# The order of work on Pool in the first half of an attention and mixture-of-experts kernel: gate bias and q spreads ahead of later loads, the k sort evacuations shared out anew, and expert pieces from unit 16

## The chip, the cores and the metric

The kernel runs on one core of a Trainium2 chip. Its time is device microseconds; the figure of a kernel is the median of its runs. The core has five engines that work side by side, each in the order of its own instructions: TensorE (PE in the profile), VectorE (DVE), ScalarE (ACT), GpSimd (POOL) and SyncE (SP). Transfers between the chip's main memory and the on-chip memory go over DMA queues; those that change the type from f32 to bf16 on the way are issued by Pool, as are the scatters of single rows.

## The reference

The input is q, k, v of shape (4, 8, 768, 64), a table `sort_net` of 8 x 8 for each of the 32 heads, and the weights of a gate and of eight experts. Cut to what matters:

```python
P = sort_net
for _ in range(5):                       # rows, then columns, are normalised
    P = exp(P - max(P)); P /= sum(P, -1); P /= sum(P, -2)
k_sorted = einsum('bhij,bhjcd->bhicd', P, k_b)   # 8 blocks of 96 rows are mixed
v_sorted = einsum('bhij,bhjcd->bhicd', P, v_b)
scores = scale * q_b @ k_sorted.T                # inside each block of 96
attn   = softmax(scores);  attn_out = attn @ v_sorted

x      = attn_out as (3072, 512)
logits = x @ w_gate + modality_bias[modality_id]
e_idx  = argmax(logits);  gate_w = softmax(logits)[e_idx]
out    = gate_w * (relu(x @ w1[e_idx]) @ w2[e_idx])   # one expert for each row
```

## The kernel before

Heads are handled in two groups of 16 (two batches each); g is 0 for the first half and 1 for the second. The whole attention is 32 *units*: unit u has one head number (u % 8) of two batches and four of the eight blocks. A unit is scores (sc), exponential (attnT), product with v (op), and division into the row buffer xb. While units run, other work is hung on them: q is spread into an interleaved layout (`spread_q`, tile q_il), transposed on TensorE (`tq_pe`, tile tq) and copied (tile qT); the rows of a finished head pair are transposed (`gate_T`, tile gt), copied (xTg), multiplied with the gate (`gate_L`, tile lg) and added up (lacc). The first of the four gate products of a group of rows also takes the gate bias, tile biasm, which `gate_bias` computes on Pool:

```python
def spread_q(g, hq, eng=None):      # two copies of 128x768, one for each of two heads
    t = q_in(g, hq // 2).rearrange(...)
    il = q_il[hq % 2].rearrange(...)
    for z in range(2):
        (eng or nc.vector).tensor_copy(il[:, z], t[...])
...
def gate_bias():
    nc.gpsimd.tensor_scalar(modN, modF, -1.0, 1.0, ALU.mult, ALU.add)
    ...
    nc.gpsimd.tensor_tensor(biasm, modF.broadcast_to([BLK, NTL, E]), bb(1), ALU.mult)
    nc.gpsimd.tensor_tensor(tmp, modN.broadcast_to([BLK, NTL, E]), bb(0), ALU.mult)
    nc.gpsimd.tensor_tensor(biasm, biasm, tmp, ALU.add)
...
def gate_L(m, c):
    lg = mipsum.tile([BLK, 8, E], FP32, tag="mi", name=f"lg{m}_{c}")
    for t in range(8):
        nc.tensor.matmul(lg[:, t], xTg[c % 2][:, t], wgp[:, c], start=True, stop=True)
    ...
    if c == 0:
        nc.vector.tensor_tensor(la..., lg..., bm, ALU.add)      # bm is a view of biasm
    else:
        nc.vector.tensor_tensor(la, la, lg, ALU.add)
```

PSUM results are copied out either by ScalarE or by VectorE. Which of the two is decided when the program is written, by a running account of work given to each: `use` adds to the account, `pick` takes the engine that would be done first, `copy_out` is a copy by the engine picked.

```python
def pick(act, dve):
    top = max(busy)
    for z in range(2):
        busy[z] = max(busy[z], top - 3.0)
    z = 0 if busy[0] + act <= busy[1] + dve else 1
    busy[z] += (act, dve)[z]
    return z == 0
...
def sort_k(g, c0, kind):            # "mi": 8 columns in a one-bank tile; "sc", "op": 16 in two banks
    ...                             # matmuls on k_raw, into tile ka
    copy_out(dst, acc..., *((0.6, 0.7) if kind == "mi" else (1.03, 1.23)))
```

The order of the first half, as it stands in the program:

```python
use(dve=0.5)
home_pick()                          # 13 small VectorE operations
mod_rows()
kinds = [s_, o_] + [m_] * 8 + ([m_] * 4 + [o_]) * 2 + [m_] * 4
g0 = jobs(0, kinds)
for f, g, x0, kd in g0[:10]:         # the k sort of the first half
    f(g, x0, kd)
scores(0); expo(0); mod_T()
load_k(1, 0); load_k(1, 1)           # k of the second half, into the buffer of the first
home_map()                           # its last part on Pool: perm_mult(BTp, ...)
gate_w()                             # Pool
spread_q(0, 1, nc.gpsimd)
use(dve=-busy[1], act=-busy[0])
for n, (f, g, x0, kd) in enumerate(g0[10:]):   # the v sort of the first half
    f(g, x0, kd)
    if n == 3:
        scores(1); expo(1)
load_v(1)
spread_q(0, 2, nc.gpsimd)
load_q(1, 0, 4); load_w(0, parts=(0,)); load_q(1, 4, 4); load_w(0, parts=(1,))
make_upper_triangular(nc, maskUT, val=1.0, diag=False)
...
prep_q(2); av(0); prep_q(3)          # prep_q: transposes of q for a unit, and their copy
```

Then the loop over the units. The lists A1 and A2 hold what is hung on a unit:

```python
at2(2, lambda: (spread_q(0, 3, nc.gpsimd), gate_bias()))
at2(3, make_bd, 1)
at2(4, late_consts)
# k and v sort of the second half: 12 and 16 jobs on units 8 to 15
for m in range(3):
    at2(8 * m + 9, place, m)         # choose expert places of 8 row tiles, scatter the rows
    at2(8 * m + 11, table_x, m)      # table of slots; x of a slot is loaded, transposed, into xT
at2(12, late_w1)                     # weights of the second expert, after x of slots 0 and 1

def pace(u):
    return (0, 0) if u < 17 else (1, u % 2)

for u in range(2, 32):
    p1, p2 = pace(u)
    scores(u); expo(u)
    run_pieces(p1)
    for f, a in A1.get(u, []): f(*a)
    av(u - 1); prep_q(u + 2); prep_s(u + 3)
    run_pieces(p2)
    for f, a in A2.get(u, []): f(*a)
run_pieces(1); av(31); run_pieces(1); gate_T(3, 3); run_pieces(1); gate_L(3, 3); choose(3)
run_pieces(1); place(3); run_pieces(1); table_x(3); run_pieces(1000)
```

A *piece* is a part of an expert's work on a slot of 256 rows: four pieces of eight matmuls for the first layer (tile hp) and two of eight for the second (tile yp). Twelve slots of six pieces and a last, smaller one make up the second stage of the kernel, and some of them are woven into the units of the second half.

Of the kernel before, what the change touches and what calls it, by code (L numbers as in the profile page):

```python
# [17 lines left out]
def kernel(  # L18
# [13 lines left out]
    nc = tc.nc  # L32
# [58 lines left out]
    def q_in(g, hh):  # L91
        base = q_in1 if g else v_sb[1].rearrange("p x d -> p (x d)")
        return base[:, hh * 3072:(hh + 1) * 3072]
# [15 lines left out]
    def load_k(g, part):  # L109
        cs = slice(part * RW // 2, (part + 1) * RW // 2)  # L110
        nc.gpsimd.dma_start(out=k_raw[:, cs], in_=k_src[g * 128:(g + 1) * 128, cs])

    def load_v(g):
        nc.gpsimd.dma_start(out=v_in, in_=v_src[g * 128:(g + 1) * 128])

    def load_q(g, h0, nh):
        t = q_in(g, h0 // 4).rearrange("p (r h f) -> p r h f", r=2, h=4)
        z = h0 % 4
        for par in range(2):
            nc.gpsimd.dma_start(out=t[:, par, z:z + nh], in_=q[2 * g + par, h0:h0 + nh]  # L120
                                .rearrange("h (p t) d -> p h (t d)", t=6))

    def spread_q(g, hq, eng=None):
        t = q_in(g, hq // 2).rearrange("p (r h t d) -> p r h t d", r=2, h=4, t=6)
        il = q_il[hq % 2].rearrange("p (h t r d) -> p h t r d", h=2, t=6, r=2)
        for z in range(2):
            (eng or nc.vector).tensor_copy(il[:, z], t[:, :, (hq % 2) * 2 + z].rearrange("p r t d -> p t r d"))  # L127
# [62 lines left out]
    def perm_mult(dst, srcs, nm):  # L190
        eng = nc.gpsimd
        tmp = small.tile([128, 4, E, E], FP32, tag="ptmp", name=f"ptmp{nm}")
        a = bass.AP(tensor=srcs.tensor, offset=srcs.offset, ap=[srcs.ap[0], srcs.ap[1], [0, E], srcs.ap[2]])
        p_ = bass.AP(tensor=perm.tensor, offset=perm.offset, ap=[perm.ap[0], [0, 4], perm.ap[1], perm.ap[2]])
        eng.tensor_tensor(tmp, a, p_, ALU.mult)
        for w in (4, 2):
            eng.tensor_tensor(tmp[:, :, :, 0:w], tmp[:, :, :, 0:w], tmp[:, :, :, w:2 * w], ALU.add)
        eng.tensor_tensor(dst.rearrange("p r (e o) -> p r e o", o=1), tmp[:, :, :, 0:1], tmp[:, :, :, 1:2], ALU.add)
# [32 lines left out]
    def tq_pe(u):  # L231
        h = u % 8
        src = q_il[(h // 2) % 2].rearrange("p (h t f) -> p h t f", h=2, t=6)[:, h % 2]
        tp = mipsum.tile([128, 6, 128], BF16, tag="mi", name=f"tq{u}")
        for t in range(6):
            nc.tensor.transpose(tp[:, t], src[:, t], ident)  # L236
        tq[u] = tp

    def tq_out(u, eng):
        g, h = u // 16, u % 8  # L240
        qT = qTb[g][:, h * 768:(h + 1) * 768].rearrange("p (i t r) -> p i t r", i=NB, t=6)
        eng(qT, tq.pop(u).rearrange("p t (i r) -> p i t r", r=16))
# [55 lines left out]
    def home_map():  # L298
        nc.vector.tensor_tensor_scan(cs_, ones8, oth, 0.0, ALU.mult, ALU.add)
        nc.vector.scalar_tensor_tensor(cs_, cs_, 1.0, oth, ALU.add, ALU.mult)  # L300
        nc.vector.tensor_tensor(cs_, cs_, ohB, ALU.add)
        hb = bass.AP(tensor=cs_.tensor, offset=cs_.offset, ap=[cs_.ap[0], [0, E], cs_.ap[1]])
        nc.vector.tensor_tensor(perm, hb, sF8.broadcast_to([128, E, E]), ALU.is_equal)
        perm_mult(BTp, BT, "b")
        nc.gpsimd.tensor_copy(etab, BTp[0:1, 3])
# [6 lines left out]
    def mod_rows():  # L312
        src = modI.rearrange("b (r t w) -> b t r w", r=16, t=6)[:, :, :, 0]
        nc.gpsimd.tensor_copy(modB, src)
# [8 lines left out]
    def gate_w():  # L323
        perm_mult(wgf, wg_sb, "w")
        nc.gpsimd.tensor_copy(wgp, wgf)

    def gate_bias():
        nc.gpsimd.tensor_scalar(modN, modF, -1.0, 1.0, ALU.mult, ALU.add)

        def bb(r):  # L330
            t = BTp[0:BLK, r]
            return bass.AP(tensor=t.tensor, offset=t.offset, ap=[t.ap[0], [0, NTL], t.ap[1]])
        tmp = small.tile([BLK, NTL, E], FP32, tag="btmp", name="btmp")
# [3 lines that stand above are left out]
# [3 lines left out]
    def use(act=0.0, dve=0.0):  # L340
        busy[0] += act
        busy[1] += dve
# [8 lines that stand above are left out]
# [28 lines left out]
    def jobs(g, kinds):  # L379
        res, c0, d0 = [], 0, 0  # L380
        for kd in kinds:
            if c0 < BLK:
                res.append((sort_k, g, c0, kd))
                c0 += 8 if kd == "mi" else 16
            else:
                res.append((sort_v, g, d0, kd))
                d0 += 4 if kd == "mi" else 8
        assert c0 == BLK and d0 == D
        return res
# [3 lines left out]
    def unit(u):  # L393
        return u // 16, (u // 8) % 2, u % 8
# [6 lines left out]
    def prep_q(u):  # L401
        if 2 <= u < 32 and not (u // 8) % 2:
            tq_pe(u)
            tq_out(u, nc.scalar.copy if pick(0.8, 0.56) else nc.vector.tensor_copy)
# [23 lines left out]
    def av(u):  # L428
        g, hf, h = unit(u)
        xt = xb[(u // 8) % 2]  # L430
        op = opsum.tile([128, 2, 512], FP32, tag="op", name=f"op{u}")
        ov = op[:, :, 0:4 * (D + 1)].rearrange("p r (j x) -> p r j x", x=D + 1)
        for par in range(2):
            for j in range(4):
                i = hf * 4 + j
                c0 = (par * 4 + j) * BLK
                nc.tensor.matmul(ov[:, par, j], attnT[u % 2][:, c0:c0 + 128],  # L437
                                 v_sb[g][0:BLK, par * 64 + h * 8 + i, 0:D + 1], start=True, stop=True)
        rs = small.tile([BLK, 2, 4, 1], FP32, tag="rs", name=f"rs{u}", bufs=2)
        nc.vector.reciprocal(rs, ov[0:BLK, :, :, D:D + 1])  # L440
        nc.vector.tensor_tensor(xt[:, :, h * D:(h + 1) * D].rearrange("p (r j) d -> p r j d", r=2),  # L441
                                ov[0:BLK, :, :, 0:D], rs.broadcast_to([BLK, 2, 4, D]), ALU.mult)
        use(dve=0.92)
# [171 lines left out]
    def zero_block():  # L615
        ins = nc.sync.dma_start(out=xs_dram[ZR:ZR + PR].rearrange("(t p) w -> p t w", t=2), in_=zsrc2)
        in_xs_group(ins.ins)
        pads.append(ins.ins)
# [125 lines left out]
    m_, s_, o_ = "mi", "sc", "op"  # L744
# [15 lines left out]
    use(dve=0.5)  # L760
    home_pick()
    mod_rows()
    kinds = [s_, o_] + [m_] * 8 + ([m_] * 4 + [o_]) * 2 + [m_] * 4
    g0 = jobs(0, kinds)
    for f, g, x0, kd in g0[:10]:
        f(g, x0, kd)
# [3 lines left out]
    load_k(1, 0)  # L770
    load_k(1, 1)
    home_map()
    gate_w()
    spread_q(0, 1, nc.gpsimd)
    use(dve=-busy[1], act=-busy[0])
    for n, (f, g, x0, kd) in enumerate(g0[10:]):
        f(g, x0, kd)
# [2 lines left out]
            expo(1)  # L780
    load_v(1)
    spread_q(0, 2, nc.gpsimd)
    load_q(1, 0, 4)
    load_w(0, parts=(0,))
    load_q(1, 4, 4)
# [1 line left out]
    make_upper_triangular(nc, maskUT, val=1.0, diag=False)  # L787
    nc.gpsimd.iota(zpad.bitcast(I32)[:, Dm // 2:Dm // 2 + 1], pattern=[[0, 1]], base=SKIP, channel_multiplier=0)
    zero_block()
    prep_q(2)  # L790
    av(0)
    prep_q(3)

    st = {"tab": -1, "x": 0, "l1": 0, "done": 0, "pos": 0}

# [21 lines left out]
    def at1(u, f, *a):  # L817
        A1.setdefault(u, []).append((f, a))

    def at2(u, f, *a):  # L820
        A2.setdefault(u, []).append((f, a))
# [7 lines left out]
    for m in range(4):  # L829
        for c in range(4):  # L830
            u = 8 * m + 2 * c + 3
# [5 lines left out]
                at1(u, gate_L, m, c)  # L837
        if m < 3:
            at1(8 * m + 9, choose, m)
    at2(2, lambda: (spread_q(0, 3, nc.gpsimd), gate_bias()))  # L840
    at2(3, make_bd, 1)
    at2(4, late_consts)
    k_at = [8] * 3 + [9] * 3 + [10] * 4 + [11] * 2
# [1 line left out]
    for u, (f, g, x0, kd) in zip(k_at + v_at, jobs(1, [m_] * 28)):  # L845
        at2(u, f, g, x0, kd)
    for m in range(3):
        at2(8 * m + 9, place, m)
        at2(8 * m + 11, table_x, m)
    at2(12, late_w1)  # L850

# [14 lines left out]
    def run_pieces(n):  # L866
        for _ in range(n):
            if st["pos"] >= len(pieces):
                return
            f, a = pieces[st["pos"]]  # L870
            if (f is mL1 and a[0] >= st["x"]) or (f is last_L1 and SL >= st["x"]):
                return
            f(*a)
            if f is mL1 and a[1] == 3:
                st["l1"] = a[0] + 1
            if f is mL2 and a[1] == 1:
                st["done"] = a[0] + 1
            x_try()
            st["pos"] += 1

    def pace(u):
        return (0, 0) if u < 17 else (1, u % 2)

    for u in range(2, 32):
        p1, p2 = pace(u)
# [10 lines left out]
            f(*a)  # L896
    run_pieces(1)
    av(31)
    run_pieces(1)
    gate_T(3, 3)  # L900
    run_pieces(1)
    gate_L(3, 3)
    choose(3)
    run_pieces(1)
    place(3)
    run_pieces(1)
    table_x(3)
    run_pieces(1000)
    assert st["pos"] == len(pieces)
# [74 lines left out]
```

The softmax here doesn't subtract the row's maximum and nothing guards it: scores larger than these inputs give would overflow.

## Time and profile before

| what | value |
|---|---|
| time, median of three runs | 243.31 us (243.28 to 244.02) |
| span of the profiled execution, first to last instruction | 207.0 us |
| mean granted TensorE clock | 0.867 of full speed |
| TensorE busy | 166.8 us, 81% of the span |
| VectorE busy | 102.1 us, 49% |
| ScalarE busy | 92.6 us, 45% |
| Pool busy | 83.5 us, 40% |
| moved by DMA | 27.66 MB, mean 134 GB/s |

The profile has the busy time of each engine, a picture of the span in 40 equal slices, and groups of instructions by line of the kernel, engine and operation. A name like "tq<-ident,q_il" gives the tile that is written and those that are read, so L236 is the transposes of q, L437 the product with v, L450 `gate_T`, L456 `gate_L`, L366 the k sort, L375 the v sort, L683 and L706 the two expert layers; on Pool L127 is `spread_q` and L328 to L336 are `gate_bias`; on VectorE L462 is the addition that takes biasm, and L441 the division into xb. The list of waits has, for an engine and a line, what it waited for, in microseconds in total, how often, and the longest. A timeline gives the start, the duration, and in square brackets how long the engine sat idle before and what released it. A table of windows has the busy time of each engine in a stretch, and near its end the granted TensorE clock, the DMA share and GB/s.

### The profile page before, as it was taken

How to read it: one execution, taken by the hardware profiler on the slowest of the kernel's cores; microseconds unless marked ns; L12 is line 12 of the kernel's file. 1: busy time of each engine (PE TensorE's matmuls, PEld its weight loads, DVE VectorE, ACT ScalarE, POOL GpSimd, SP SyncE). 2: the span in 40 equal slices, each digit the busy share in tenths (PEclk: the TensorE clock that was granted, in tenths of full speed). 3: DMA queues.
4: the chain of work that ended last, by engine and by line, in shares of the span. 5: the costliest groups of instructions: out<-in, count | busy, mean ns of one | idle time of the engine just before them, and what ended most of it. 6: DMA issues, size and time to landing. Idle time of an engine off the chain costs nothing.

```text
span 207.0 us, 5130 instructions
## 1 busy us (share of the span) xinstructions
PE 166.8 (81%) x2034; PEld 121.8 (59%) x2045; DVE 102.1 (49%) x333; ACT 92.6 (45%) x148; POOL 83.5 (40%) x118
## 2 busy tenths in 40 slices
PE   6395497438899998999978999889999999999100
PEld 2135496327698887768657586648676767654000
DVE  5969377255484866864638453572222322223000
ACT  2035368325575797759435674434232223232000
POOL 7901377930007603177241773257631313132300
PEclk9859679755555799999999999999999999999955
DMA  4999999999993326998550226963577321212200
GB/s 54 207 228 205 194 221 196 204 186 211 205 190 81 88 54 57 165 181 215 152 153 3 77 80 184 177 172 110 165 186 187 83 103 51 101 55 101 62 2 0
DMA packets 30160, 27.66 MB, mean 134 GB/s; under 512 B 18831, under 2 KB 25775, under 8 KB 29872
## 3 DMA queue, kind: packets, MB, share of 16 engines
q0 software_dynamic: 11792, 23.10, 51.0%
q1 hardware_dynamic: 18336, 4.16, 11.3%
q8 instruction: 18, 0.29, 0.6%
q14 instruction: 14, 0.11, 0.2%
HBM read 27.35 MB, written 10.52 MB: 183 GB/s over the span
## 4 chain that ended last, share of the span: by engine, by line
PE 60%; issue 10%; POOL 9%; DVE 9%; DMA 4%; ACT 2%; POOLq 0%; DVEq 0%
PE yp L706 20%; PE hp L683 18%; PE gt L450 4%; DMA kvb<-in_k_dram 4%; PE sc L418 3%; PE lg L456 3%; PE op L437 3%; PE ka L366 3%; DVE xb L441 2%; POOL q_il L127 2%; PE va L375 2%; POOL q_in L120 1%; ACT v_sb L353 1%; PE tq L236 1%; PE ypl L736 1%
## 5 line engine op out<-in xcount | busy, mean ns | idle before, releaser
L683 PE MATMUL hp<-xT,w 128*128 128x256 bf16 x384 | 47.3, 273 | 0.1
L527 POOL DMA_INDIRECT xs_scratch<-xb,dest x32 | 29.6, 926 | 38.8 <-issue 37.9
L697 POOL DMA_INDIRECT out_dram<-kvb,idg x25 | 24.5, 982 | 42.9 <-DVE kvb L695 22.0
L683 PEld LDWEIGHTS <-w 128*128 128x128 bf16 x384 | 36.1, 98 | 7.4
L424 ACT ACTIVATE attnT<-sc 96x768 bf16<-96x768 f32 x32 | 25.9, 808 | 10.4 <-PE sc L418 10.1
L441 DVE TENSOR_TENSOR xb<-op,rs 96x512 bf16<-96x512 f32 x32 | 22.0, 686 | 1.2
L706 PE MATMUL yp<-w,qT 128*128 128x512 bf16 x91 | 22.3, 380 | 0.3
L706 PE MATMUL yp<-w,hT 128*128 128x512 bf16 x90 | 21.9, 380 | 0.3
L693 ACT ACTIVATE kvb<-yp,idg 128x512 f32<-128x512 f32 x14 | 9.6, 687 | 20.5 <-PE yp L706 20.5
L695 DVE TENSOR_SCALAR kvb<-yp,idg 128x512 f32<-128x512 f32 x10 | 7.5, 751 | 19.1 <-PE yp L706 17.2
L437 PE MATMUL op<-v_sb,attnT 96*128 96x65 bf16 x256 | 14.9, 206 | 0.7 <-DVE xb L441 0.4
L677 ACT ACTIVATE hT<-hp 128x512 bf16<-128x512 f32 x17 | 10.1, 594 | 11.5 <-PE hp L683 11.2
L450 PE MATMUL gt<-ident,xb 96*128 96x96 bf16 x128 | 9.4, 225 | 7.2 <-DVE xb L441 6.8
L677 ACT ACTIVATE qT<-hp 128x512 bf16<-128x512 f32 x15 | 9.0, 597 | 12.4 <-PE hp L683 12.1
L706 PEld LDWEIGHTS <-hT 128*128 128x128 bf16 x96 | 9.0, 98 | 9.0
L706 PEld LDWEIGHTS <-qT 128*128 128x128 bf16 x96 | 9.1, 98 | 9.0
L437 PEld LDWEIGHTS <-attnT 96*128 96x128 bf16 x256 | 12.3, 106 | 2.8 <-DVE xb L441 0.6
L418 PE MATMUL sc<-qT,kT 64*128 64x96 bf16 (+1 forms) x256 | 12.8, 226 | 1.3 <-ACT kT L353 0.7
L236 PE MATMUL tq<-ident,q_il 128*128 128x128 bf16 x96 | 9.2, 242 | 5.7 <-POOL q_il L127 5.7
L375 PE MATMUL va<-bd,kvb 128*128 128x128 bf16 x128 | 13.8, 278 | 0.0
L366 PE MATMUL ka<-bd,kvb 128*64 128x64 bf16 x384 | 10.0, 220 | 4.3 <-issue 2.0
L375 PEld LDWEIGHTS <-kvb 128*128 128x128 bf16 x128 | 12.8, 191 | 0.3
(179 smaller groups left out, 225.6 us busy)
## 6 DMA issues: line engine op xcount, KB each, us to landing
w<-in_moe_w_dram POOLq DMA_DIRECT2D x4, 1024.0 KB, 8.3
kvb<-in_k_dram POOLq DMA_DIRECT2D x4, 768.0 KB, 9.6
kvb<-in_v_dram POOLq DMA_DIRECT2D x2, 1536.0 KB
q_in<-in_q_dram POOLq DMA_DIRECT2D x4, 384.0 KB, 21.4
xs_scratch<-zpad SPq DMA_DIRECT2D x3, 258.0 KB, 3.3
v_sb<-in_q_dram POOLq DMA_DIRECT2D x4, 192.0 KB, 4.1
v_sb<-in_q_dram POOLq DMA_DIRECT2D x2, 384.0 KB, 21.5
xs_scratch<-xb,dest POOLq DMA_INDIRECT x32, 2.4
```

Of the source, the lines that this page charges most:

```text
L366: nc.tensor.matmul(acc[par * 64:(par + 1) * 64, z], k_raw[:, (c0 + z) * D:(c0 + z + 1) * D], bd[g][:, par * 64:(par + 1) * 64], start=True ...
L375: nc.tensor.matmul(acc[:, z], v_cols[:, d0 + z], bd[g], start=True, stop=True)
L418: nc.tensor.matmul(sc[0:m, par, j * BLK:(j + 1) * BLK], kT[g][rows, x0:x0 + m], qT[rows, i], start=True, stop=True)
L424: mark[0] = nc.scalar.activation(attnT[u % 2][:, 0:8 * BLK].rearrange("p (r f) -> p r f", r=2), sc_tiles.pop(u)[0:BLK, :, 0:4 * BLK], ACT. ...
L437: nc.tensor.matmul(ov[:, par, j], attnT[u % 2][:, c0:c0 + 128], v_sb[g][0:BLK, par * 64 + h * 8 + i, 0:D + 1], start=True, stop=True)
L441: nc.vector.tensor_tensor(xt[:, :, h * D:(h + 1) * D].rearrange("p (r j) d -> p r j d", r=2), ov[0:BLK, :, :, 0:D], rs.broadcast_to([BLK, ...
L450: nc.tensor.transpose(tp[:, t], xb[m % 2][:, t, c * 128:(c + 1) * 128], ident[:BLK, :BLK])
L527: ins = nc.gpsimd.indirect_dma_start(out=xs_dram, out_offset=bass.IndirectOffsetOnAxis(ap=dest[:, t:t + 1], axis=0), in_=xt.bitcast(I32)[: ...
L677: mark[0] = nc.scalar.activation(dst, src, ACT.Relu)
L683: nc.tensor.matmul(hp[:, f], w_at(s, c * F + (2 * j + f) * 128, 128), xT_b[s % NX][:, c], start=(c == 0), stop=(c == 3))
L697: ins = nc.gpsimd.indirect_dma_start(out=out, out_offset=bass.IndirectOffsetOnAxis(ap=idg[:, t, 0:1], axis=0), in_=y, in_offset=None, boun ...
L706: nc.tensor.matmul(yp, hT_b[s % 2][:, fc, t * 128:(t + 1) * 128], w_at(s, 4 * F + fc * Dm, Dm), start=(fc == 0), stop=(fc == 7))
```

## The change

It has four parts.

1. On Pool, `gate_bias()` and the last spread of q of the first half, `spread_q(0, 3)`, go from unit 2 to a place ahead of the loads of q and of expert weights for later, so that they don't queue behind the issuing of those loads. `prep_q(2)`, `av(0)` and `prep_q(3)` are written ahead of them, because the last spread reuses a buffer that `prep_q(3)` reads. `spread_q(0, 1)` goes ahead of `gate_w()`.
2. In the k sort of the first half, `use(dve=1.6)` tells the account that VectorE has `home_pick` to do, and one of the two large jobs goes from second to sixth place, so that the copies are shared more evenly.
3. Expert pieces begin with unit 16 and not with unit 17.
4. `place(2)` goes from the end of unit 25 into unit 26, after its scores and one expert piece; after the units some of the single pieces between the steps of the last group become two.

```diff
-    kinds = [s_, o_] + [m_] * 8 + ([m_] * 4 + [o_]) * 2 + [m_] * 4
+    use(dve=1.6)
+    kinds = [s_] + [m_] * 4 + [o_] + [m_] * 4 + ([m_] * 4 + [o_]) * 2 + [m_] * 4
...
     home_map()
+    spread_q(0, 1, nc.gpsimd)
     gate_w()
-    spread_q(0, 1, nc.gpsimd)
...
     load_v(1)
     spread_q(0, 2, nc.gpsimd)
+    gate_bias()
+    prep_q(2)
+    av(0)
+    prep_q(3)
+    spread_q(0, 3, nc.gpsimd)
     load_q(1, 0, 4)
     load_w(0, parts=(0,))
...
     zero_block()
-    prep_q(2)
-    av(0)
-    prep_q(3)
...
-    at2(2, lambda: (spread_q(0, 3, nc.gpsimd), gate_bias()))
...
     for m in range(3):
-        at2(8 * m + 9, place, m)
+        if m == 2:
+            at1(26, place, m)
+        else:
+            at2(8 * m + 9, place, m)
...
-        return (0, 0) if u < 17 else (1, u % 2)
+        return (0, 0) if u < 16 else (1, u % 2)
...
     run_pieces(1)
     av(31)
-    run_pieces(1)
+    run_pieces(2)
     gate_T(3, 3)
     run_pieces(1)
     gate_L(3, 3)
     choose(3)
-    run_pieces(1)
+    run_pieces(2)
     place(3)
-    run_pieces(1)
+    run_pieces(2)
     table_x(3)
```

## The prediction

> **What bounds the kernel now.** I read the picture in 40 slices first, then the waits between 34 and 46 us, then Pool's and TensorE's timelines there, last a table of windows for the clock.
>
> ```profile
> PE   6395497438899998999978999889999999999100
> POOL 7901377930007603177241773257631313132300
> PEclk9859679755555799999999999999999999999955
> DMA  4999999999993326998550226963577321212200
> ```
>
> A slice is 5.18 us. From slice 14 (72 us) on TensorE is nearly full at full clock: what comes before that moves the end one for one. Slices 7 and 8 (36 to 47 us) are almost empty and, from there to slice 12, the clock is half. The DMA engines are full from slice 1 to slice 11 (62 us). The waits of that stretch:
>
> ```profile
> DVE lacc L462 <- POOL biasm L336: 6.0, 1, 6.0
> PE gt L450 <- DVE xb L441: 3.7, 2, 3.5
> PE tq L236 <- POOL q_il L127: 2.5, 1, 2.5
> ```
>
> All three lead to Pool. VectorE waits 6.0 us for the gate bias; the division into xb behind it in VectorE's order is late, so TensorE waits 3.5 us for xb; before that it has waited 2.5 us for the spread of q. Pool in that time waits for nothing:
>
> ```profile
> 32.84 1.60 POOL L127 COPY q_il<-v_sb 128x768 bf16<-128x768 bf16 x2
> 34.37 1.50 POOL L120 DMA_DIRECT2D q_in<-in_q_dram  x2
> 35.86 0.76 POOL L638 DMA_DIRECT2D w<-in_moe_w_dram  x1
> 36.59 1.51 POOL L120 DMA_DIRECT2D q_in<-in_q_dram  x2
> 38.05 0.93 POOL L640 DMA_DIRECT2D w<-in_moe_w_dram  x1
> ...
> 39.61 1.58 POOL L127 COPY q_il<-v_sb 128x768 bf16<-128x768 bf16 x2
> ...
> 42.65 0.72 POOL L336 TENSOR_TENSOR biasm<-biasm,btmp 96x256 f32<-96x256 f32 x1
> ```
>
> It issues six loads for later, then builds constants, and only then spreads and computes the bias. What this does to TensorE:
>
> ```profile
> 40.48 0.82 PE L236 MATMUL tq<-ident,q_il 128*128 128x128 bf16 x6 [2.55 <-POOL q_il L127]
> 41.23 0.50 PE L418 MATMUL sc<-qT,kT 64*128 64x96 bf16 x8
> 45.23 0.82 PE L450 MATMUL gt<-ident,xb 96*128 96x96 bf16 x8 [3.49 <-DVE xb L441]
> ```
>
> And the clock, in windows of about 3.4 us (first number busy TensorE, the third from the end the clock):
>
> ```profile
> 32.40:35.80 3.40, 2.44 (x52) 2.06 (x53) 2.25 (x5) 2.57 (x5) 3.40 (x5) 1.00 1.09 197
> 35.80:39.20 3.40, 2.06 (x44) 1.63 (x41) 1.35 (x3) 2.14 (x3) 3.40 (x6) 1.00 1.00 196
> 39.20:42.60 3.40, 1.25 (x14) 0.85 (x14) 0.00 (x0) 0.77 (x1) 3.30 (x7) 0.50 0.95 174
> ...
> 63.10:66.60 3.50, 3.29 (x62) 2.90 (x61) 1.88 (x5) 1.19 (x2) 2.79 (x3) 0.50 0.34 93
> 66.60:70.00 3.40, 3.40 (x41) 3.16 (x41) 2.55 (x12) 2.87 (x6) 2.50 (x3) 0.51 0.30 86
> ```
>
> The clock falls at 39.2 us, after a window with 2.06 us of work that ends in the first gap. It doesn't come back until 70 us, although TensorE is then busy nearly all the time: only the v sort, with its 128-wide matmuls, brings it back. So the cost of the gap is 6.0 us at once and a half clock for units 5 to 12.
>
> [...] falls and rises stand at 8.5, 15.3, 22.1, 29.0, 39.2 and 70.0 us, on a grid of 3.4. [...] here 2.06 us of 3.40 busy was followed by one, so the measurement sets the limit, between 2.06 and 2.44 us busy for this mix. [...] the trace shows 0.75 to 0.93 us of Pool for each. [...] One division of P_t took 1.29 us beside a spread at 9.06 us (0.21 otherwise); but the 0.69 us of xb beside the spread at 32.84 us was not stretched, and I put nothing for it.
>
> **The change, part by part.**
>
> *Pool's order.* After the spread that ends at 34.44 us, gate bias takes 0.21 + 0.61 + 0.61 + 0.72 with their gaps = 2.2 us, so biasm stands at 36.6 us and not at 43.4. The last spread follows: first half at 37.4 (40.4 before), all at 38.2. Its buffer is free, the transposes of unit 3 being done at 33.4. The first gate product ends at 37.2 us, so VectorE no longer waits; TensorE's own order ends at 37.9 us, so the transposes no longer wait either. Gain at once: 2.55 + 3.49 = 6.0 us. Moving `spread_q(0, 1)` gains nothing: it ended at 30.4 us and its transposes ran at 31.8, behind the v sort.
>
> *The later loads.* They are issued 3.8 us later, from 38.2 us. By then the slices of the DMA row have moved 1305 GB/s x 5.18 us + 0.4 = 7.2 MB; q of the first half and all of k and v are 7.9 MB, so 0.7 MB or about 3.5 us are still queued. The engines don't run dry and the last weight load still lands at about 61.5 us.
>
> *The clock.* The window to 39.2 us now has about 0.7 us more work (2.75) and should stay warm. The next, units 5 and 6, I count as 2.3 us from the durations at full clock (gt 0.35, op 0.27, tq 0.35, lg 0.4, sc 0.3, op 0.27, sc 0.3), right between the limits, and units 7 and 8 as about 2.1 us. Three cases for where unit 16 starts (78.7 us before):
>  - it falls where it fell: 6.3 us earlier, the gap alone (chance 0.2);
>  - it falls at about 46 us: units 5 to 7 take 5.7 us for 7.3 (10.8 less the 3.5 of the gap), so 6.3 + 1.6 = 7.9 us (0.45);
>  - it stays: units 8 to 12 took 15.6 us at half clock; the two copying engines have 9.6 us there, units 12 to 16 took 2.75 us each at full clock, so 11 us, 4.5 less, 12.4 in all (0.35).
>
> *The limit behind the last case.* [...] scatter number eight of the first rows waits for the last weight load, 61.5 us, and goes out at 62 (70.56 before). From its start to the landing of the first slot's x are 6.2 us (to 73.39, and 3.4 to landing), so the first piece can't start before 68.2 us, and unit 17 not before some 70.2: 10.7 us earlier at most. Weights: 0.2 x 6.3 + 0.45 x 7.9 + 0.35 x 10.7 = 8.6 us.
>
> *The k sort.* By the account the copies were ScalarE one large and five small, VectorE one large and three small, behind `home_pick`, which ends at 18.9 us. Now ScalarE has both large and four small ones, 4.5 us from 16.9 us, VectorE four small ones. Before, the seventh small job waited for a copy that VectorE began after its large one (20.0 us), and matmuls resumed at 20.71; now that copy is its first, done at 19.5. But after 28 matmuls TensorE stops from 21.3 to 23.3 us with nothing named, and the last copy ends at 24.2. I don't know whether this stop moves along; 0.4 us of 1.1.
>
> *Pieces and places.* In the second half the waits of TensorE are the three for places (1.8 us together, of which 0.71 and 0.68 are touched) and 0.70 for the last table, which pieces now cover: 2.1 us. A piece in unit 16 takes about 1 us, of which the 0.68 us wait there covers most, and saves it at the end. Some new waits will stay: 1.7 us together.
>
> Sum: 8.6 + 0.4 + 1.7 = 10.7 us; 243.3 - 10.7 = 232.6 us.
>
> **The rivals.**
>  - *The loads are what it really waits for.* If the later issue lets the DMA run dry, everything of the second half is late. Against it: 0.7 MB queued; k of the second half is issued earlier anyway, and q of it is read at 72 us. For it: only 2 us of slack. It would leave 4 to 6 us of gain, 238.
>  - *The clock falls all the same and only the gap goes.* For it: the light units 6 and 7. Then 243.3 - 6.3 - 0.4 - 1.7 = 234.9.
>  - *Second-half work becomes the bound*: pieces from unit 16 reach x before it has landed, since its scatter hangs on the loads. That is the limit above; it caps the best case at 230.5. If weights of the second expert (issued after x of slot 1, 81.1 us before, some 8.3 us to landing) are late as well, one or two more are lost.
>  - *Places later, tables later*: `place(2)` a piece later delays slot 4 by some 2 us while PE reaches it about two pieces earlier. Its x was issued at 124.2 us and used at 132; the 8 us less 3.4 to landing hold. Nothing.
>
> **Range and chances.** The cases of the clock stand 4.4 us apart, the tail and the k sort add 1.5 either way: 229.0 to 236.5 us. A gain of 2% needs 238.4 us; only the first rival comes near. Faster 0.93, within 2% 0.06, slower 0.01.
>
> **What would show it.** Right: no wait of lacc on biasm, none of tq on the spread near 38 us, biasm done at about 36.6; slices 7 and 8 filled; unit 16 at 68 to 72 us; the rk and cp waits gone. The clock row tells which case holds. Wrong: a hole in the DMA row near 42 us, TensorE waiting for x at its first piece longer than 2 us, or a half clock already at 39 us.

## The result and the profile after

| | time, median | range |
|---|---|---|
| kernel before, 4 runs beside it | 243.52 us | 243.28 to 244.02 |
| changed kernel, 4 runs | 236.73 us | 235.68 to 237.31 |
| ratio | 0.9714 | 95% interval 0.9674 to 0.9753 |

The change takes 6.8 us off. Predicted were 10.7 us and 232.6 us; the result lies just above the range, at 229.0 to 236.5.

First, the picture of the changed kernel in 40 slices, 5.87 us each here:

```profile
PE   6583987796289899049898059999749999999500
POOL 7801879206600307700307710206731332233300
PEclk9979799555569999659999555999958999999955
DMA  5999999999707696350202273313537522212200
```

It looks unlike the page of before: TensorE has holes at slices 10, 16, 22 and 29, counted from 0, at none of which before had one. The list of waits has a new entry (total, times, longest):

```profile
ACT attnT L424 <- remote: 21.9, 3, 9.4
```

and ScalarE's timeline (start, duration, in brackets the idle time before it and what released it) has two of the three:

```profile
101.98 0.81 ACT L424 ACTIVATE attnT<-sc 96x768 bf16<-96x768 f32 x1 [9.42 <-remote]
136.69 0.81 ACT L424 ACTIVATE attnT<-sc 96x768 bf16<-96x768 f32 x1 [9.34 <-remote]
```

ScalarE waits over 9 us for scores that TensorE has long computed by its own record. For the first of these two, TensorE's timeline has them at

```profile
91.82 0.34 PE L418 MATMUL sc<-qT,kT 64*128 64x96 bf16 x8
```

"remote" says that the profile has no releaser for the wait. I call this a stop. The page of before, on which the prediction rests, has a span of 207.0 us and no stops, although its time is 243.31 us; I passed over those 36 us. The runs were made in sessions (the expectations say "call"), and in a session either every kernel had the stops (the kernel before then takes 243.5 to 246.2 us) or none had (206.1 to 206.7 us), so I compare only within a session. The sessions of e1 and of e8 ran on the same chip by its number on record, the one with stops and the other without, so it isn't the chip alone; what it is isn't known. A trace of the kernel before taken in a session with stops (e1_before, a slice is 6.05 us) has them too, at slices 10 and 11, 17, 22 and 23, and 28:

```profile
PE   7574982679319989709979429979169999999600
```

So they don't make the difference; the change is worth 6.7 to 7.7 us without them and 6.8 to 7.0 with them.

The page that answers to that of before is therefore the changed kernel in a session without stops (run e18_after, span 197.1 us, a slice is 4.93 us):

```profile
PE   6587398877998979999799997999999999999000
POOL 7911197970077021675405772067733132232300
PEclk9969669975589999999999999999999999999755
DMA  3999999999998549985901339936297912112200
```

The two nearly empty slices at 36 to 47 us are gone. From there on four slices (8 to 11, 39 to 59 us) have a lowered clock, for seven before. The DMA row is full without a hole to slice 11 (59 us). Pool's timeline shows the new order:

```profile
35.28 0.72 POOL L336 TENSOR_TENSOR biasm<-biasm,btmp 96x256 f32<-96x256 f32 x1
35.95 1.59 POOL L127 COPY q_il<-v_sb 128x768 bf16<-128x768 bf16 x2
37.48 1.60 POOL L120 DMA_DIRECT2D q_in<-in_q_dram  x2
39.07 0.75 POOL L638 DMA_DIRECT2D w<-in_moe_w_dram  x1
...
54.36 1.01 POOL L527 DMA_INDIRECT xs_scratch<-xb,dest  x1 [11.36 <-issue]
...
63.35 0.97 POOL L527 DMA_INDIRECT xs_scratch<-xb,dest  x1 [0.61 <-DMA w<-in_moe_w_dram]
```

The gate bias stands at 36.0 us (predicted 36.6, before 43.4), the spreads at 37.5 us (38.2). The loads come after them. The eighth scatter of the first rows waits for a weight load as predicted, 0.61 us here, 0.63 in e5 and 1.13 in e6, and goes out at 63.35 us (70.56 before; predicted 62). In the trace of before the profile names no load ahead of it (0.31 us idle), so that it would wait for one was my estimate; why it is the eighth isn't shown. TensorE's timeline:

```profile
37.16 0.50 PE L236 MATMUL tq<-ident,q_il 128*128 128x128 bf16 x6
37.93 0.35 PE L418 MATMUL sc<-qT,kT 64*128 64x96 bf16 x8 [0.27 <-ACT attnT L424]
38.57 0.51 PE L450 MATMUL gt<-ident,xb 96*128 96x96 bf16 x8 [0.29 <-DVE xb L441]
```

The transposes no longer wait for Pool (2.55 us before), and the gate product waits 0.29 us for xb where it waited 3.49.

### The profile page after: what moved, and what is told of

It is laid out like the page before. It is cut to its first block, busy times and chain, and to the rows that moved or that the text cites. A ratio compares the mean times of both kernels' runs of the same rounds, so it can differ in the third digit from the quotient of the medians.

```text
span 234.8 us, 5146 instructions
## 1 busy us (share of the span) xinstructions
PE 174.2 (74%) x2045; PEld 125.0 (53%) x2045; DVE 102.0 (43%) x333; ACT 93.0 (40%) x148; POOL 83.6 (36%) x118
## 4 chain that ended last, share of the span: by engine, by line
PE 60%; DVE 12%; another core or an unknown queue 10%; issue 6%; ACT 6%; POOL 1%; POOLq 0%; ACTq 0%; DVEq 0%
PE yp L706 18%; PE hp L683 17%; PE va L375 4%; PE sc L418 4%; PE op L437 4%; PE gt L450 3%; PE lg L456 3%; PE ka L366 3%; DVE xb L441 2%; ACT attnT L424 2%; ACT v_sb L353 2%; DVE kT L353 1%; DVE hT L675 1%; DVE P_t L272 1%
## 5 line engine op out<-in xcount | busy, mean ns | idle before, releaser
L683 PE MATMUL hp<-xT,w 128*128 128x256 bf16 x384 | 51.4, 287 | 0.5 <-ACT hT L677 0.5
L683 PEld LDWEIGHTS <-w 128*128 128x128 bf16 x384 | 37.7, 102 | 10.4 <-issue 1.7
L706 PE MATMUL yp<-w,qT 128*128 128x512 bf16 x96 | 24.8, 405 | 4.0 <-ACT hT L677 4.0
L418 PE MATMUL sc<-qT,kT 64*128 64x96 bf16 (+1 forms) x256 | 12.9, 226 | 17.5 <-ACT attnT L424 16.6
L706 PE MATMUL yp<-w,hT 128*128 128x512 bf16 x96 | 22.5, 379 | 0.0
L418 PEld LDWEIGHTS <-kT 64*128 64x128 bf16 (+1 forms) x256 | 7.9, 103 | 19.8 <-issue 18.0
L695 DVE TENSOR_SCALAR kvb<-yp,idg 128x512 f32<-128x512 f32 x11 | 8.3, 751 | 21.6 <-PE yp L706 21.6
L440 DVE RECIPROCAL rs<-op 96x8 f32<-96x8 f32 x32 | 6.3, 198 | 22.5 <-PE sc L418 7.4
L693 ACT ACTIVATE kvb<-yp,idg 128x512 f32<-128x512 f32 x13 | 8.9, 687 | 17.0 <-PE yp L706 14.7
L456 PE MATMUL lg<-wgp,xTg 128*96 128x8 bf16 x128 | 9.2, 195 | 7.1 <-issue 6.0
L456 PEld LDWEIGHTS <-xTg 128*96 128x96 bf16 x128 | 8.8, 141 | 9.3 <-issue 6.2
```

Source lines behind the costliest of these rows:

```text
L418: nc.tensor.matmul(sc[0:m, par, j * BLK:(j + 1) * BLK], kT[g][rows, x0:x0 + m], qT[rows, i], start=True, stop=True)
L683: nc.tensor.matmul(hp[:, f], w_at(s, c * F + (2 * j + f) * 128, 128), xT_b[s % NX][:, c], start=(c == 0), stop=(c == 3))
L693: nc.scalar.activation(dst, src, ACT.Copy, scale=gate)
L706: nc.tensor.matmul(yp, hT_b[s % 2][:, fc, t * 128:(t + 1) * 128], w_at(s, 4 * F + fc * Dm, Dm), start=(fc == 0), stop=(fc == 7))
```

## The experiments

Eighteen runs in five sessions: e1 to e4 and e12 to e15 with stops, e5 to e7, e8 to e11 and e16 to e18 without. "Before" is the kernel before in the same session, and ratios are to it. Times are medians of all executions, while ratios and intervals leave out those more than 1.5% above the fastest of the same kernel, which would move a median by 0.9 us at most (e17: 203.78).

| run | what | time us | before us | ratio, 95% |
|---|---|---|---|---|
| e1_before | nothing changed | 244.47 | 244.61 | 1.0027, 0.9996 to 1.0057 |
| e2_pool_order | part 1 alone | 237.58 | 244.61 | 0.9747, 0.9665 to 0.983 |
| e3_rest | parts 2 to 4 | 243.0 | 244.61 | 0.9926, 0.9895 to 0.9956 |
| e4_pool_ksort | parts 1 and 2 | 237.78 | 244.61 | 0.9744, 0.9672 to 0.9817 |
| e5_double_scatter | change, 8 scatters twice | 213.46 | 206.7 | 1.0297, 1.0218 to 1.0375 |
| e6_split_scatter | change, 4 + 4 scatters | 204.15 | 206.7 | 0.9858, 0.9775 to 0.9941 |
| e7_paced_scatter | change, scatters one by one | 205.16 | 206.7 | 0.9907, 0.9871 to 0.9942 |
| e8_after | change | 199.76 | 206.43 | 0.9682, 0.9632 to 0.9732 |
| e9_double_scatter | as e5 | 213.06 | 206.43 | 1.0319, 1.0246 to 1.0393 |
| e10_split_scatter | as e6 | 204.31 | 206.43 | 0.9888, 0.9854 to 0.9921 |
| e11_pool_ksort | parts 1 and 2 | 200.45 | 206.43 | 0.9725, 0.9682 to 0.9768 |
| e12_fill2 | change, 2 spare matmuls per unit | 237.08 | 246.18 | 0.9642, 0.9587 to 0.9697 |
| e13_fill4 | change, 4 spare matmuls | 242.16 | 246.18 | 0.9865, 0.9826 to 0.9905 |
| e14_after | change | 239.16 | 246.18 | 0.9756, 0.9706 to 0.9805 |
| e15_double_scatter | as e5 | 252.06 | 246.18 | 1.026, 1.0194 to 1.0326 |
| e16_fill2 | as e12 | 199.54 | 206.08 | 0.9651, 0.9564 to 0.9738 |
| e17_fill2_paced | e12 and e7 together | 204.72 | 206.08 | 0.9885, 0.9851 to 0.9919 |
| e18_after | change | 198.37 | 206.08 | 0.9576, 0.9498 to 0.9654 |

### Which part brings it: e1 to e4, e8 and e11

The edits are the parts of the change itself: e2 has only the diff of part 1, e4 and e11 add that of part 2, e3 has everything but part 1, e1 nothing. For e11, seen from the whole change:

```diff
-        if m == 2:
-            at1(26, place, m)
-        else:
-            at2(8 * m + 9, place, m)
+        at2(8 * m + 9, place, m)
...
-        return (0, 0) if u < 16 else (1, u % 2)
+        return (0, 0) if u < 17 else (1, u % 2)
...                                   # and run_pieces(2) back to run_pieces(1), three times
```

> The kernel before once more, unchanged, to see what an execution of some 243 us looks like in a trace. Theory A (stops): the missing 36 us between the 207 us span and the 243 us time are stops [...] as in the trace of the changed kernel (four of them, about 28 us); a trace of 243 us then has them too, some 30 to 38 us in sum, and the units up to 10 start as in the first trace. Theory B (brought by the change): the kernel before has no such stops; a trace shows 207 us again and the rest of the 243 us lies outside the span.

> Part 1 alone: gate bias and the last spread of q ahead of the later loads on Pool. Both theories: the exponential of unit 10 starts about 6.8 us earlier than before (8.0 with all parts, of which 1.2 stood already at unit 0 and came from the k sort). Theory A: the time falls by 6 to 8 us, to 236 or 237, if the stops stay as long as they are before. Theory B: the time falls by less than 3 us, or rises, because the work that moved earlier is what brings the stops.

> Everything but part 1: k sort sharing, pieces from unit 16, place and the pieces at the end. Units 0 to 10 start 1.2 us earlier, and the half clock from 39 to 70 us stays. Theory A: 1.2 plus up to 1.7 us, so 240 to 242.5. Theory B (stops come from expert pieces that start before their scatters and loads are through): the time stays or rises, 243 to 247.

> Parts 1 and 2 without parts 3 and 4. Theory A: unit 10 starts 8.0 us earlier; the time is 235 to 237.5, within 2 us of the whole change, since parts 3 and 4 give at most 1.7. Theory B: without the earlier pieces the stops go, and the time is 228 to 233, well under that of the whole change.

> The whole change, unchanged, in one call with three others. The kernel before took 244.6 us in the first call of experiments and 206.7 in the second[...]. If this call has the stops (before near 244): ratio 0.970 to 0.975, units 0 to 16 about 8 us earlier. If it has none (before near 207): theory G (the gain of the first half is 7 to 8 us in both, and what follows gives part of it back waiting for x of slot 2): 202 to 203.5 us, ratio 0.978 to 0.985, and a wait of TensorE for x of the third slot of 1 to 3 us. Rival H (all of the predicted sum comes through where there are no stops): 196 to 198 us.

> Parts 1 and 2 without the earlier pieces and the later place (237.8 us with stops). Theory G: pieces from unit 16 and the new end are worth nothing or less where TensorE then waits for x: without stops this kernel is within 1 us of the whole change, 202 to 204; with stops within 1 us too. Rival P (parts 3 and 4 pay as predicted): it is 1.5 to 2 us slower than the whole change in the same call.

Part 1 alone is 7.0 us shorter than before (244.61 - 237.58), in a session with stops; parts 1 and 2 are 6.8 us there and 6.0 in a session without. The whole change is 6.7 us in the latter, so pieces and places add 0.7 us (200.45 - 199.76; the runs of both overlap). Without part 1 the others make 1.6 us, with stops.

Against the expectations: e1 and e2 came out as theory A said. e3 lies 0.5 us above the range of A, and its unit 0 begins 0.7 us later than in e1, not 1.2 earlier; e4 is 0.3 us above its range. e8 lies between the ranges of G and H. e11 is within 1 us of the whole change, as G said, but below the 202 to 204 us given.

The k sort adds nothing that can be seen: e4 is 0.2 us longer than e2. TensorE's timeline of the k sort, first before, then the changed kernel (e18_after):

```profile
16.81 2.56 PE L366 MATMUL ka<-bd,kvb 128*64 128x64 bf16 x119
20.71 0.63 PE L366 MATMUL ka<-bd,kvb 128*64 128x64 bf16 x28 [1.34 <-DVE kT L353]
23.30 0.32 PE L366 MATMUL ka<-bd,kvb 128*64 128x64 bf16 x4 [1.96 <-issue]
```

```profile
16.81 2.33 PE L366 MATMUL ka<-bd,kvb 128*64 128x64 bf16 x104
19.35 0.63 PE L366 MATMUL ka<-bd,kvb 128*64 128x64 bf16 x28 [0.21 <-DVE kT L353]
22.47 0.32 PE L366 MATMUL ka<-bd,kvb 128*64 128x64 bf16 x4 [2.49 <-issue]
```

The wait for VectorE's copy is gone and the 28 matmuls come 1.36 us earlier, but the stop after them, for which the profile names no releaser, grows from 1.96 to 2.49 us. In this pair 0.64 us are left when the softmax of the first unit begins (24.20 for 24.84 us). In the seventeen traces with part 2 it begins at 23.72 to 25.03 us, in the three without it (before, e1, e2) at 23.53 to 24.84: the scatter is larger than what was to be gained.

Pieces and places: the list of waits of e11 and then of e18 (engine, line and what it waited for; total, times, longest).

```profile
PE rk L498 <- DVE oh L482: 1.8, 3, 0.7
```

```profile
PE hp L683 <- DMA xT<-xs_scratch: 1.7, 2, 1.4
```

The three waits for places are gone from TensorE's list, as meant. A wait of nearly the same sum stands there instead: first-layer pieces that reach x of a slot before it has landed, 0.33 us at the first slot and 1.41 us at the fifth (slot 4, whose rows `place(2)` sends). The last matmul ends at 183.87 us in e11 and at 183.92 in e8.

### Scatters: e5, e6, e7, e9, e10, e15 and e17

Each stop lies beside a burst of eight row scatters, 1.22 us apart; in the changed kernel the bursts begin at 53.79, 87.64, 123.72 and 161.97 us. Do the stops follow the scatters (S in the expectations of e15 and e17), or do they come at fixed places of the program (F)? e5 sends the eight scatters of the second block of units twice:

```diff
         for t in range(8):
             one(t)
+        if m == 1:
+            for t in range(8):
+                nc.gpsimd.nop()
+                one(t)
```

e6 sends four of them three units later, and the table of slots at unit 21; e7 sends one per half unit from unit 17 on (e7 shown):

```diff
-        for t in range(8):
+        for t in range(1 if m == 1 else 8):
...
-        at2(8 * m + 11, table_x, m)
+        at2(8 * m + 11 + (2 if m == 1 else 0), table_x, m)
+    at1(18, lambda: [ones_[1](t) for t in (1,)])
+    at2(18, lambda: [ones_[1](t) for t in (2,)])
...                                   # and so on to unit 21
```

> The changed kernel, but the eight row scatters of the second group of rows (places of m = 1) go out twice, the same rows to the same places. Theory S (scatter): the stops[...] last as long as scatters follow each other 1.2 us apart; the stop between units 19 and 20, 9 to 10 us long in the changed kernel, becomes 18 to 20 us and the time rises by 8 to 10 us, to 245 to 247. Theory F (fetch, or another place in the program): the stop belongs to the program's position or to the table and the slot loads that follow; it keeps its 9 to 10 us, and the time stays within 2 us of 236.7.

> The changed kernel, but of the same eight scatters four go out in unit 17 and four not before the end of unit 20, with the table of that group two units later. Theory S: the stop begins only after the third or fourth scatter of a burst, so two bursts of four cost 1 to 4 us instead of 9 to 10, and the time falls to 229 to 233. If every scatter costs its share, two stops of 4 to 5 us, 235 to 238. Theory F: one stop of 9 us, moved with the table or not, 236 to 238.

> The changed kernel, but of the same eight scatters one goes out in unit 17 and one with every half unit after it, some 1.5 to 1.7 us apart instead of 1.2. Theory S: if the stop is a queue that fills because scatters come faster than something drains, a longer spacing shortens it below 4 us and the time falls to 229 to 233; if each scatter holds the updates back for its own 1.2 us, the stop is the same 9 us in sum and the time 236 to 238. Theory F: 9 us, 236 to 238.

> The changed kernel with the eight row scatters of the second group sent twice, as once before in a call without stops (213.5 us there, with TensorE waiting 9.6 us for x of slot 2). If this call has stops: theory S (a stop lasts as long as scatters follow each other): the stop after unit 19 is 18 to 20 us instead of 9 to 10, time 244 to 247; theory F (bound to the program's position): 9 to 10 us and the time within 2 us of the whole change. If it has none: 8 to 10 us above the whole change, again by the wait for x.

> The changed kernel with the second group's scatters in two bursts of four, the second at the end of unit 20, and its table two units later (204.15 us without stops). If this call has stops: theory S with a threshold (they begin with the third or fourth scatter): two stops of under 3 us each, time 3 to 6 us under the whole change; theory S with a share for each scatter: two of 4 to 5 us, the same time. Theory F: one stop of 9 us in the old place. If it has none: 0.5 to 2.5 us above the whole change, because x of slot 2 comes later.

> The change with the second group's row scatters sent twice. Where this call has stops: theory S, the stop after unit 19 becomes 18 to 20 us, 244 to 247 us; theory F, it keeps 9 to 10 us and the time stays within 3 us of the whole change. Where it has none: 12 to 14 us above the whole change, as measured twice, with the wait of TensorE for x of slot 2.

> As e16, with the eight row scatters of the second block of units sent one per half unit instead of all at once. Theory S (a long stop goes with a burst of scatters): where the stops are there, the stop after unit 19 is gone, three are left, and the time is 4 to 9 us under e16. Rival F (the stops come at a fixed place of the program whatever the scatters do): four stops, and the time is within 1 us of e16 or longer. Where no stops are there, both expect 3 to 5 us over e16, the wait for the rows of a later slot that the paced run showed before.

e5 to e7 fell into a session without stops and told nothing of them, but something else: later or longer scatters are on the path at once. In e9, 13.3 us over the whole change in the same session (213.06 - 199.76), TensorE's timeline has

```profile
107.14 1.89 PE L687 MATMUL hp<-xT,w 128*128 128x256 bf16 x8 [9.03 <-DMA xT<-xs_scratch]
```

a 9.03 us wait for x of a later slot, whose rows are behind the second sending. Split scatters cost 4.6 us in that session (204.31 - 199.76), and with the spare matmuls the paced ones cost 4.2 (203.78 - 199.54), with the same kind of wait (2.85 and 2.77 us at the same slot). So there is hardly any slack left between the placing of rows and the pieces that use them. Expected were 8 to 10 us for e9, 0.5 to 2.5 for e10 and 3 to 5 for e17.

e15 fell into a session with stops. Pool's first and last scatter, TensorE's scores and ScalarE's softmax of them, first in e14_after, then in e15:

```profile
89.01 0.98 POOL L527 DMA_INDIRECT xs_scratch<-xb,dest  x1 [8.99 <-issue]
...
93.20 0.34 PE L418 MATMUL sc<-qT,kT 64*128 64x96 bf16 x8
...
97.63 0.91 POOL L527 DMA_INDIRECT xs_scratch<-xb,dest  x1 [0.30 <-issue]
...
103.47 0.81 ACT L424 ACTIVATE attnT<-sc 96x768 bf16<-96x768 f32 x1 [8.03 <-remote]
```

```profile
89.84 0.98 POOL L527 DMA_INDIRECT xs_scratch<-xb,dest  x1 [9.12 <-issue]
...
94.02 0.34 PE L418 MATMUL sc<-qT,kT 64*128 64x96 bf16 x8
...
108.17 0.91 POOL L527 DMA_INDIRECT xs_scratch<-xb,dest  x1 [0.30 <-issue]
...
114.81 0.81 ACT L424 ACTIVATE attnT<-sc 96x768 bf16<-96x768 f32 x1 [19.25 <-issue]
```

With sixteen scatters ScalarE's idle time grows from 8.03 to 19.25 us, and the softmax follows its scores by 20.5 us (114.81 - 94.36) instead of 9.9 (103.47 - 93.54). It is over 5.7 us after the last scatter's 0.91 us (114.81 - 109.08), in e14 4.9 us (103.47 - 98.54). The stop follows the length of the burst, then, and isn't tied to a place in the program. It is the timeline that shows this, in one pair of traces; the time doesn't. e15 takes 12.9 us more than e14 (252.06 - 239.16), above the 244 to 247 us of theory S, and doubling the burst cost as much where there were no stops (13.3 us in e9). What in the burst makes ScalarE start late, and why only in some sessions, isn't settled. Whether pacing removes a stop wasn't seen: e17 was to show it, and its session had none.

### The clock: e12, e13, e14, e16 and e18

The prediction gave its largest gain to a clock that stays full. In every kernel with part 1 and no spare matmuls it falls at 40.8 to 43.4 us, about one window later than before (39.2). Two spare matmuls per unit are to keep it full; e13 has four. Their result is not read.

```diff
+        if 4 <= u <= 11:
+            fill = mipsum.tile([128, 512], FP32, tag="mi", name=f"fill{u}")
+            for z in range(2):
+                nc.tensor.matmul(fill, ones_bf, wsrc, start=True, stop=True)
```

> The whole change plus spare work for the clock: at the end of each of units 4 to 11 two matmuls of 512 columns on constant data, whose result nothing reads [...]. In all traces with part 1 the clock fell at 40.8 to 43.4 us and came back at 53.6 to 56.6. Theory C (the half clock is what holds units 6 to 12): the clock stays full or falls later, units 8 to 12 take 11 to 12.5 us instead of 14.5, unit 16 starts 2 to 4 us earlier than with the change alone, and the time is 1.5 to 3.5 us under it. Theory E (VectorE and ScalarE hold these units anyway, and the spare matmuls stand in the way): the clock stays but units 8 to 12 keep 14 us or more, and the time is the same within 1 us or longer by up to 2.

> The same with four spare matmuls in each of units 4 to 11[...]. Theory C: the clock surely stays full; unit 16 as with two or 0.5 to 1.5 us later, because the spare work now fills more than the idle time; time 0.5 to 3 us under the whole change. Theory E: 1 to 4 us longer than the whole change.

> The whole change in the same call, for comparison: ratio to before 0.965 to 0.976 in any case; 199 to 201 us where there are no stops, 235 to 238 where there are. If there are stops, their number is four, each beside a burst of eight row scatters.

> Theory C (the first half is worth less than predicted because the TensorE clock still falls at about 41 us): the two spare matmuls per unit take away that fall, and the whole change plus spare matmuls is 2 to 3 us shorter than the whole change where the long stops of TensorE are there (part of the gain is given back in the stop after unit 11), and 3 to 5 us shorter where they are not. Rival theory (the spare matmuls gain by chance of where the stops fall, not by the clock): without stops it is no shorter than the whole change, or up to 1.5 us longer, the added work.

> The whole change, unchanged, as the control of the two others in the same call: 0.964 to 0.978 of the kernel before; with stops 236 to 240 us, without 199 to 201 us.

With stops e12 was 2.1 us shorter than the whole change (237.08 for 239.16), as if the clock had been the missing term. But unit 11 of e12 began 4.6 us earlier than in e14 and unit 12 only 1.4: it had just slipped in ahead of the first stop. The runs without stops decide. The table of windows, busy TensorE first and the clock third from the end, e18 and then e16:

```profile
31.70:35.10 3.40, 2.35 (x49) 1.97 (x50) 2.35 (x6) 2.57 (x5) 3.40 (x6) 1.00 1.14 231
35.10:38.50 3.40, 2.84 (x60) 2.30 (x57) 2.93 (x10) 2.37 (x4) 3.32 (x6) 1.00 0.98 209
38.50:41.90 3.40, 2.44 (x52) 2.08 (x54) 2.84 (x15) 2.97 (x4) 3.40 (x5) 0.99 0.95 198
41.90:45.30 3.40, 3.12 (x47) 2.59 (x44) 1.93 (x5) 0.98 (x2) 1.02 (x5) 0.50 1.25 195
...
52.10:55.50 3.40, 3.40 (x97) 2.99 (x93) 2.54 (x11) 2.99 (x6) 1.01 (x1) 0.50 1.29 203
55.50:58.90 3.40, 3.00 (x78) 2.68 (x74) 2.33 (x6) 1.92 (x5) 2.62 (x3) 1.00 1.26 207
```

```profile
43.30:46.70 3.40, 1.98 (x37) 1.23 (x35) 2.37 (x6) 1.16 (x2) 0.00 (x0) 0.99 1.24 184
46.70:50.10 3.40, 3.40 (x66) 2.27 (x65) 0.86 (x2) 1.78 (x3) 0.00 (x0) 0.50 1.14 233
50.10:53.50 3.40, 2.88 (x91) 2.20 (x88) 2.52 (x11) 2.50 (x5) 0.00 (x0) 1.00 1.17 214
53.50:56.90 3.40, 2.60 (x86) 1.89 (x86) 2.22 (x8) 2.26 (x5) 1.70 (x2) 1.00 1.28 198
```

In e16 the clock is half for one window, 46.7 to 50.1 us, in e18 for four, 41.9 to 55.5. Yet e16 takes 199.54 us and e18 198.37, and unit 16 begins at 71.59 us in e16 and 70.05 in e18. So the rival's forecast came true: without stops the spare matmuls gain nothing, and their 2.1 us with stops can't be put down to the clock. e17 says the same, where the clock is not lowered between 28 and 99 us (a slice is 5.04 us):

```profile
PEclk9969979999999999999859999999999999999955
```

Its unit 16 begins at 70.00 us. What a full clock is worth here can be estimated. From unit 8 to unit 12 e18 takes 14.24 us; e16 takes 15.59, of which four pairs of spare matmuls are 2.8 (0.59 to 1.03 us each). Without them some 12.8 would be left, so about 1.4 us, by an estimate. In this stretch e18 has 10.4 us of half clock (45.1 to 55.5) and e16 3.4, so that is 1.4 us for 7.0. e17 takes 14.48 us, of which four pairs at 0.59 us are 2.4, so 12.1 without them, 2.1 us less than e18 for 10.4 us. Both come to 0.2 us for each us at half clock, some 3.1 for the 15.6 us of before, where the prediction had 4.5. Both take the spare matmuls at their whole length; where they fill time in which TensorE would have waited, the half clock costs less still. At full clock, in e16 from 50.1 us on, TensorE is busy 2.88 and 2.60 us of a window, spare matmuls included, and idle for the rest; at half clock, in e18 at 52.1 us, it is busy all of it. Part of what the lower clock takes comes out of time in which TensorE would have waited.

Four spare matmuls (e13) cost 3.0 us against e14, within theory E's 1 to 4. e14 lies 1.2 us above its range of 235 to 238 us, e18 0.6 us below its 199 to 201.

## Why the prediction was off, by its own steps

**Pool's order, the gap of 6.0 us: right.** Bias, spreads, transposes and gate product are where the prediction put them, within 0.7 us, and both waits are gone. In e18 the softmax of unit 6 begins at 40.92 us and not at 48.31, 7.4 us earlier, 0.6 of which are there at unit 0 already.

**The loads: right that they don't run dry, late by 2 to 4 us at the end.** DMA stays full and TensorE's first piece waits 0.33 us for x. But the last weight load was to land at 61.5 us; the eighth scatter, where it waits for this load, goes out at 63.35 us in e18, 64.91 in e11 and 65.30 in e16.

**The clock: the step that failed.** The first half was to give 8.6 us, 6.3 for the gap and 2.3 for the clock. By the medians parts 1 and 2 give 6.0 us without stops and 6.8 with them: the gap, and little or nothing for the clock. The cases were a fall where it fell (0.2), at 46 us (0.45), none (0.35). It fell between the first and the second, at 40.8 to 43.4 us, in every one of these kernels without spare matmuls, so the third case, which lent the term 0.35 x (10.7 - 7.9) = 1.0 us, didn't come. It was also priced too high: units 8 to 12 were thought to take 4.5 us more at half clock than at full, and by the estimates from e16 and e17 it is some 3.1 at most. That only the v sort brings the clock back didn't hold either: in e18 it is full from 55.5 us on, and the first matmul of the v sort is at 57.88.

The rest is in the trace that the cases were read from. Counted from unit 0 to unit 16 the first half became 7.7 us (e8), 7.6 (e11) and 8.5 (e18) shorter than in the trace of before, about what the second case said, and 7.8 (e2) and 8.5 (e4) shorter than in e1's. But the trace of before had more half clock to give back than that kernel usually has. The two tables of windows above have a clock of 0.50 or of 0.99 to 1.00. Span and mean clock are on record for every execution, and with a clock that is either half or full 2 x span x (1 - clock) is the time at half clock, an estimate: 55 us in the trace of before, 37 to 54 in 61 executions of that kernel without stops, with medians of 44 to 46 by session. Among these the span grows by 0.14 to 0.19 us for each us at half clock (a line fitted in each of the three sessions). The two go together; that the clock is the cause isn't shown by this.

**The limit at 68.2 us for the first piece: nearly two us too early.** With the late weight load the first piece begins at 70.27 us in e18, after its 0.33 us for x, and at 69.87 in e17 without a wait. By the prediction's own steps (unit 17 two us later, at 80.9 us before) that leaves some 9 us for the third case and not 10.7, an estimate, even if the clock had stayed full.

**The k sort: 0.4 predicted, nothing found**, within a scatter of 1.3 us. The stop that I couldn't explain moves along and grows.

**Pieces and places: 1.7 predicted, 0.7 found**, in runs that overlap. The waits for places went, as said. "Some new waits will stay" was counted as 0.4 us and is 1.7 us for x, about as much as the 1.8 us that went. Most of it is the fourth rival, which was put at nothing: x of slot 4 was said to be used at 132 us, 8 us after its issue at 124.2. In the trace of before the first piece of slot 4, its seventeenth of the first layer, is

```profile
129.03 1.04 PE L683 MATMUL hp<-xT,w 128*128 128x256 bf16 x8
```

4.8 us after the issue, of which the landing took 4.2. So there were 0.6 us to spare; with `place(2)` later and the pieces earlier TensorE waits 1.36 us (e8) and 1.41 us (e18) there, and in e11, with the old places, not at all.

Summed from the trace of before, e8 and e18 are 8.6 and 9.0 us shorter from unit 0 to the last matmul; by the medians the change is worth 6.7 to 7.7. The trace of before is of an execution of 208.62 us, while the medians of that kernel without stops are 206.1 to 206.7: about 2 us, as much as the difference. Its 10 us more at half clock, at 0.14 to 0.19 us each, would be 1.4 to 1.9 of them, an estimate. I took one trace as if it were the median. So of the 3.9 us that are missing some 1.5 come from this trace, 1.0 from the third case, 1.0 from the pieces and 0.4 from the k sort, an estimate within the scatter of the runs.

Of the rivals, the loads running dry has the number nearest to the result (238) but not the cause: the DMA row shows no hole. "Only the gap goes" had 234.9 us, nearer than my sum; it was 1.8 us too low mostly because it kept the k sort and the full tail, 2.1 us together, of which 0.7 were found.

No version beats the changed kernel in both kinds of session: spare matmuls gain 2.1 us in one and lose 1.2, within the scatter of the runs, in the other.

## What to carry to other kernels

Work out first which engine's queue order holds the first consumer back; issuing transfers for later ahead of small work for now cost 6 us here, and moving the small work ahead returned all of it. A half clock cost some 0.2 us for each us of it here, by estimates, in a stretch in which TensorE at full clock is busy 2.60 and 2.88 us of 3.40 (e16): look at this busy share before pricing a half clock. And check that the execution of the profile is as long as the times beside it and has their clock, or the page explains another run than the one to be predicted.

## What the runs showed of the hardware

- Stops: in some sessions TensorE has a hole beside each burst of eight row scatters 1.22 us apart, four in a run. At two of them ScalarE begins 9.8 and 9.5 us after the scores end by TensorE's record (changed kernel, 92.16 to 101.98 us and 127.24 to 136.69); ScalarE's idle time beside a single burst reaches 10.88 us (e14, up to 140.37 us). The kernel before takes 244.6 us with the stops and 206.4 without. Doubling a burst lengthens ScalarE's idle time from 8.03 us (e14) to 19.25 (e15). The cause is open.
- A half clock cost some 0.2 us for each us of it: 1.4 us for 7.0 (e16 against e18) and 2.1 us for 10.4 (e17 against e18), by estimates, in a stretch in which TensorE at full clock is busy 2.60 and 2.88 us of 3.40 (e16).
- The fall of the clock isn't set by the busy share of one window. In e18 a window with 2.44 us of 3.40 busy is the last before a fall and one with 2.35 is not; before, one with 2.44 was not. The limit that the prediction set between 2.06 and 2.44 doesn't hold, and it didn't in its own trace: from 104.1 to 107.5 us TensorE is busy 1.97 us there, and the clock stays full (1.00 in this window and in the next). Falls and rises stand a multiple of about 3.4 us apart (in e18 at 41.9 and 55.5 us by the table above, and at 28.2 by the mean clock of 0.88 from 25.0 to 38.5 us). No idle window came before a fall in the two tables above: the falls follow windows with 2.44 (e18) and 1.98 us (e16) busy.
